# Tokens multiplied by VectorE, the place of their weights, and a range check in a fused convolution and MLP kernel

## The chip, the core and the metric

The kernel runs on one core of one Trainium2 chip. The metric is the device time of one execution in microseconds (us). Before the change it is 745.89 us, the median of three runs (745.74 to 745.92).

The core's engines have queues of their own and work through them in order: TensorE (PE, with PEld for the weight load that precedes a matmul), VectorE (DVE), ScalarE (ACT), GpSimd (POOL) and SyncE (SP, which only issues DMAs here). They meet through semaphores.

## The reference

Two stages, in fp32. A dynamic convolution: each of 8 batches x 4096 tokens has 192 values in 8 groups of 24, and for each group 7 weights, made by a softmax, that weigh the token and the six before it. Then an MLP with g = h - tanh(h).

```python
w = np.exp(weight_gen - np.max(weight_gen, axis=-1, keepdims=True))
w = w / (np.sum(w, axis=-1, keepdims=True) + 1e-09)
...
out = np.einsum('bshk,bskhg->bshg', w, x_unf)     # 7 taps
...
h = x @ w_in            # 32768 x 192  @  192 x 2048
g = h - np.tanh(h)
return (g @ w_out)      # 32768 x 2048 @ 2048 x 192
```

The weights going into the softmax are drawn as 0.3 times a normal variable. The kernel before the change leaves the maximum out and takes exp as it is.

## The kernel before

**Superblocks.** The 32768 tokens are cut into 32 superblocks of 1024: 128 partitions with 8 consecutive tokens each (j = 0 to 7). Each goes through the same stages, and the stages of several superblocks overlap. The main loop (L707) runs over n = 1 to 31, and within it over 16 tiles f of the hidden dimension (L713). `tc.manual_schedule()` (L564) keeps each engine's instructions in the order in which the code issues them, so the order is written by hand.

**Softmax.** ScalarE takes exp of the weights (L169), VectorE sums over the 7 taps (L183), takes the reciprocal (L198, into a corner of a PSUM tile) and scales (L229). For superblocks 3 and 8 GpSimd does the scaling.

**Products of the taps.** Taps 0 to 3 go to `pa`, 4 to 6 to `pb`, bf16, [taps, 8 tokens, 192]. GpSimd makes nearly all (L299). The dictionary `HELP` (L51) names *helped tokens*: (m, f) in `HELP[k]` says that while superblock m runs its tile f, VectorE makes taps 0 and 1 of one token of superblock k (`help`, L243), starting with j = 7, and GpSimd's first product of k gets shorter by a token. Superblocks 4 to 31 have one such token, at f = 3 two superblocks ahead; 9 to 14 have a second, at f = 12 three ahead. VectorE first copies the 16 weights of the token into the PSUM tile `ph` of that f (L250), whose values have been used by then, and multiplies from there (L251).

**Adding the taps.** A DMA that accumulates adds `pb` onto taps 0 to 2 of `pa` (L236). For the superblocks in `TWO_SUMS` (13 to 31) a second such DMA adds taps 2 and 3 onto 0 and 1. What is left is added by TensorE: matmuls against an identity transpose the parts and add them up in PSUM (`pc`, L384), 24 for each part in each superblock, 96 with four parts and 48 with two. ScalarE evicts the result to `convT` (L410).

**First matmul.** For each f, six matmuls (three chunks of 64 channels by two halves of the tokens) write `ph` (L427), [128, 1024] fp32, two PSUM banks; there are three such buffers, shared with `pc`. ScalarE makes `th` = tanh (L440), VectorE `gt` = `ph` - `th` in bf16 (L441).

**Second matmul.** It lags one superblock. A block is one token column j of 128 tokens, and takes 32 matmuls (16 tiles, two row halves of 64) into one of two PSUM banks, `obank` 0 and 1, alternately, columns 0 to 191 of 512 (L495). `out_stream` interleaves the first half of block i with the second half of block i - 1, in pairs; `out_pairs(m)` emits m pairs. How many come after each f stands in the lists `pairs` of the plans (L682 to L686): `STEADY` has 0 after f = 2 and 16 after f = 3, 0 after f = 8 and 6 after f = 9, 8 after each of f = 11 to 14. Superblocks 4 to 11 use `DOUBLE`, with the same numbers at f = 2, 3 and 8. ScalarE evicts a finished block to `out_sb` (L514), and SyncE stores eight together.

**The end.** The second matmul of superblock 31 has nothing to run beside (`gemm2_last`, L529): for each of its eight blocks 32 matmuls into a `ph` buffer, a ScalarE copy of one half (L551) and a VectorE add of the other (L552); SyncE stores two blocks at a time (L554).

Of the kernel before, what the change touches and what calls it, by code (L numbers as in the profile page):

```python
# [8 lines left out]
FP32 = mybir.dt.float32  # L9
# [3 lines left out]
AX = mybir.AxisListType  # L13


@with_exitstack
def kernel(
# [18 lines left out]
    J = 8  # L36
# [9 lines left out]
    TWO_SUMS = (13, 14, 15, 16, 17, 18, 19, 20, 21, 22, 23, 24, 25, 26, 27, 28, 29, 30, 31)  # L46
# [4 lines left out]
    HELP = {n: ((n - 2, 3),) for n in (4, 5, 6, 7, 8, 9, 10, 11, 12, 13, 14, 15, 16, 17, 18, 19, 20, 21, 22, 23, 24, 25, 26, 27, 28, 29, 30, 31)} | {9: ((7, 3), (6, 12)), 10: ((8, 3), (7, 12)), 11: ((9, 3), (8, 12)), 12: ((10, 3), (9, 12)), 13: ((11, 3), (10, 12)), 14: ((12, 3), (11, 12))}  # L51
    LAST_TAP = (4, 5, 6, 7, 8)
    X_LATE = ()
    ZERO_AT = 8
# [28 lines left out]
    once = const.tile([P, 1], FP32, name="once")  # L83

# [94 lines left out]
    def softmax_sum(n, j0=0, j1=J):  # L179

        if j0 == 0:
            zsum_of[n] = wgpool.tile([P, J * H], FP32, name="zsum")
        nc.vector.reduce_sum(  # L183
            out=zsum_of[n][:, j0 * H : j1 * H],
            in_=e_of[n][:, j0:j1].rearrange("p j h k -> p (j h) k"),
            axis=AX.X,
        )

# [5 lines left out]
    def softmax_norm(n, bank):  # L194

        wsm = softmax_tile()
        zr_v = bank[:, 512 - J * H : 512]
        nc.vector.reciprocal(zr_v, zsum_of[n][:])  # L198

        def finish():  # L200
            scale(nc.vector, wsm[:], e_of[n], zr_v)

        wsm_of[n] = (wsm, None, None, None)
        return finish

    def softmax_norm_ramp(n, bank):
# [4 lines left out]
        nc.vector.reciprocal(zr_v, zsum_of[n][:])  # L211
# [31 lines left out]
    def help(n, ph, j):  # L243

        if n not in held:
# [3 lines left out]
        w = ph[:, 0, 0 : KH * H].rearrange("p (k h) -> p k h", k=KH)  # L249
        nc.vector.tensor_copy(w, wsm[:, j].rearrange("p h k -> p k h")[:, 0:KH])  # L250
# [7 lines left out]
            w.rearrange("p k (h o) -> p k h o", o=1).to_broadcast([P, KH, H, G]),  # L258
# [269 lines left out]

    def gemm2_last(j, f0=0, f1=NFT):  # L529

        n = NTOT - 1
        if f0 == 0:
            half[j] = psum_h.tile([P, 2, HT], FP32, name="po2", tag="ph")
        po = half[j]
        col = (j % 2) * HT + (j // 2) * P
        for f in range(f0, f1):
            for r in range(2):
                nc.tensor.matmul(  # L538
                    po[:, r, 0:D],
                    lhsT=g_of[n][f][r * R : (r + 1) * R, col : col + P],  # L540
                    rhs=w_out[r * R : (r + 1) * R, f, :],
                    start=(f == 0),
                    stop=(f == NFT - 1),
                )
        if f1 < NFT:
            return
# [4 lines left out]
        nc.scalar.activation(out=ot[:], in_=po[:, 0, 0:D], func=ACT.Copy)  # L551
        nc.vector.tensor_add(out_sb[:, j, :], po[:, 1, 0:D], ot[:])  # L552
        if j % 2 == 1:
            nc.sync.dma_start(  # L554
                out=out[n * TOK : (n + 1) * TOK, :].rearrange("(p j) e -> p j e", p=P)[
                    :, j - 1 : j + 1, :
                ],
                in_=out_sb[:, j - 1 : j + 1, :],
            )
# [4 lines left out]
    ctx.enter_context(tc.manual_schedule())  # L564
# [122 lines left out]
    DOUBLE_IN = (4, 5, 6, 7, 8, 9, 10, 11)  # L687
# [19 lines left out]
    for n in range(1, NTOT):  # L707
# [5 lines left out]
        for f in range(NFT):  # L713
            ph = gemm1(n, f)
# [17 lines left out]
            if n == AHEAD and f == 4:  # L732
                softmax_exp(n + 4)
            if n > 1:
# [9 lines left out]
            for m in (n + 2, n + 3):  # L744
                if (n, f) in HELP.get(m, ()):
                    help(m, ph, J - 1 - HELP[m].index((n, f)))
# [22 lines left out]

    gemm2_last(0, 0, J)  # L770
    out_pairs(NFT)
    gemm2_last(0, J, NFT)
    for j in range(1, J):
        gemm2_last(j)

# [29 lines left out]
```

## Time and profile before

| what | value |
|---|---|
| median of three runs | 745.89 us |
| span of the profiled execution, first to last instruction | 743.4 us |
| superblocks 8 to 11 (four parts), from tanh to tanh | 22.67 us each |
| superblocks 14, 15, 17, 18 (two parts) | 21.85 us each |
| subtraction L441, VectorE | 512 x 1217 ns |
| tanh L440, ScalarE | 512 x 1025 ns |
| copy of a helped token's weights L250, VectorE | 34 x 190 ns |
| product of a helped token L251, VectorE | 34 x 554 ns |
| GpSimd's first product with 8, 7, 6 tokens | 6025, 5416, 4765 ns |
| accumulating DMA, issue on POOL: first, second sum | 1284, 1651 ns |
| last matmul's end in the span | 739.57 us |

The profile is of one execution, and its span is 2.5 us under the median time of the runs; what lies before the first and after the last instruction is not in it. How to read its lines: a group or timeline line gives the source line, the engine, the operation, output <- inputs by their names, shapes and a count, and where the engine idled before it, how long and what ended that. A line of waits gives who waited, for whom, the sum in us, how often, and the longest. A line of windows gives the stretch, its length, busy time and count for each engine, the clock granted to TensorE (1.00 is full), the busy share of the DMA engines and GB/s.

### The profile page before, as it was taken

Reading aid. Unit: us, or ns where it says so; the run is one execution under the profiler, and the core shown is the slowest. Engines: PE = TensorE matmul, PEld = TensorE weight load, DVE = VectorE, ACT = ScalarE, POOL = GpSimd, SP = SyncE. Lnnn points to the kernel's source line nnn. Section 1 sums busy time; section 2 is a strip of 40 time slices with the busy share of each in tenths; the row PEclk is TensorE's granted clock in tenths of the full one; section 3 lists DMA queues with packets and bytes.
Section 4 is the critical chain, followed back from the end, with each engine's and each line's share of the span. In section 5 each row is a group of like instructions: output and inputs, shape, how many; then the busy total and the mean of one; then the engine's idle time right before and its main releaser. Section 6 shows DMA issues by size and latency. Waiting matters only on the chain.

```text
span 743.4 us, 30037 instructions
## 1 busy us (share of the span) xinstructions
PE 722.3 (97%) x13616; PEld 556.5 (75%) x13616; DVE 687.4 (92%) x723; ACT 638.8 (86%) x872; POOL 654.5 (88%) x163
## 2 busy tenths in 40 slices
PE   3899999999999999999999999999999999999997
PEld 2477777778777777777777777777777777877777
DVE  7999899999999999999999999999999999988893
ACT  4888888888888888989889999898998989888882
POOL 7999999999999999999999999999999999991000
PEclk9899999999999999999999999999999999999999
DMA  8925367766567668878777977877887877776112
GB/s 236 245 46 161 135 172 185 195 179 149 124 183 184 183 185 224 210 199 203 166 202 209 236 186 204 178 195 205 221 209 195 192 181 194 193 149 110 45 45 86
DMA packets 34269, 130.06 MB, mean 175 GB/s; under 512 B 4591, under 2 KB 9439, under 8 KB 30174
## 3 DMA queue, kind: packets, MB, share of 16 engines
q0 software_dynamic: 19424, 51.12, 40.4%
q1 hardware_dynamic: 14718, 77.03, 27.6%
q8 instruction: 106, 1.74, 0.9%
q14 instruction: 21, 0.17, 0.1%
HBM read 54.52 MB, written 25.17 MB: 107 GB/s over the span
## 4 chain that ended last, share of the span: by engine, by line
PE 92%; DVE 5%; ACT 1%; issue 1%; DMA 1%; SPq 0%; DVEq 0%
PE ph L427 43%; PE obank L495 43%; PE pc L384 4%; DVE gt L441 3%; PE po L538 1%; ACT th L440 1%; DVE pa L299 1%; DMA wg_t<-in_weight_gen_dram 1%; DVE zsum L183 0%; SPq L134 0%; ACT convT L402 0%; DVE obank L211 0%; DVE pa L251 0%; DVE pb L299 0%; SPq L144 0%
## 5 line engine op out<-in xcount | busy, mean ns | idle before, releaser
L441 DVE TENSOR_TENSOR gt<-ph,th 128x1024 bf16<-128x1024 f32 x512 | 601.6, 1217 | 33.4 <-ACT th L440 23.2
L440 ACT ACTIVATE th<-ph 128x1024 f32<-128x1024 f32 x512 | 512.1, 1025 | 69.2 <-PE ph L427 60.3
L427 PE MATMUL ph<-convT,w_in 64*128 64x512 bf16 x3072 | 415.1, 379 | 5.3 <-DVE gt L441 3.3
L495 PEld LDWEIGHTS <-gt 64*128 64x128 bf16 x7936 | 355.6, 94 | 80.6 <-issue 6.3
L495 PE MATMUL obank<-w_out,gt 64*128 64x192 bf16 x7936 | 408.0, 243 | 0.9 <-issue 0.8
L299 POOL TENSOR_TENSOR pa<-x_t,wsm 128x2688 bf16<-128x2688 f32 (+3 forms) x68 | 338.9, 5232 | 0.2
L299 POOL TENSOR_TENSOR pb<-x_t,wsm 128x4608 bf16<-128x4608 f32 (+2 forms) x33 | 283.8, 8601 | 0.7 <-ACT wsm L221 0.5
L427 PEld LDWEIGHTS <-w_in 64*128 64x128 bf16 x3072 | 163.0, 94 | 86.0 <-issue 18.3
L514 ACT ACTIVATE out_sb<-obank 128x192 f32<-128x192 f32 x248 | 81.3, 328 | 11.2 <-PE obank L495 10.3
L410 ACT ACTIVATE convT<-pc 128x1024 bf16<-128x1024 f32 (+1 forms) x62 | 50.1, 810 | 2.9 <-PE pc L384 2.7
L236 POOL DMA_DIRECT2D pa<-pb x28 | 36.0, 1284 | 13.7 <-POOL pb L299 9.1
L384 PEld LDWEIGHTS <-pa 64*128 64x128 bf16 x2064 | 41.5, 100 | 6.8 <-DVE pa L299 1.1
L236 POOL DMA_DIRECT2D pa<-pa x21 | 34.7, 1651 | 9.6 <-DMA pa<-pb 8.9
L384 PE MATMUL pc<-ident,pa 64*128 64x64 bf16 x1968 | 41.2, 191 | 1.8 <-POOL pa L299 0.9
L183 DVE TENSOR_REDUCE zsum<-wg_t 128x32 f32<-128x224 f32 (+1 forms) x61 | 23.6, 387 | 2.9 <-ACT wg_t L169 2.9
L169 ACT ACTIVATE wg_t<-wg_t 128x448 f32<-128x448 f32 x32 | 18.2, 570 | 6.3 <-DMA wg_t<-in_weight_gen_dram 6.2
L251 DVE TENSOR_TENSOR pa<-x_t,ph 128x384 bf16<-128x384 f32 x34 | 18.8, 554 | 2.0 <-DVE ph L250 0.3
L229 DVE TENSOR_TENSOR wsm<-wg_t,pc 128x448 f32<-128x448 f32 x27 | 16.8, 621 | 2.5
L198 DVE RECIPROCAL pc<-zsum 128x64 f32<-128x64 f32 x27 | 14.9, 550 | 0.0
L384 PE MATMUL pc<-ident,pb 64*128 64x64 bf16 x216 | 4.9, 206 | 9.0 <-POOL pb L299 9.0
L384 PEld LDWEIGHTS <-pb 64*128 64x128 bf16 x288 | 6.3, 106 | 9.5 <-POOL pb L299 9.0
L538 PE MATMUL po<-w_out,gt 64*128 64x192 bf16 x256 | 11.2, 243 | 0.0
(27 smaller groups left out, 56.8 us busy)
## 6 DMA issues: line engine op xcount, KB each, us to landing
x_t<-in_x_dram SPq DMA_DIRECT2D x31, 1344.0 KB, 7.9
pa<-pb POOLq DMA_DIRECT2D x28, 1152.0 KB, 9.5
out_dram<-out_sb SPq DMA_DIRECT2D x31, 768.0 KB, 3.9
pa<-pa POOLq DMA_DIRECT2D x21, 768.0 KB, 7.2
wg_t<-in_weight_gen_dram SPq DMA_DIRECT2D x32, 224.0 KB, 7.1
x_t<-in_x_dram SPq DMA_DIRECT2D x1, 768.0 KB
w_out<-in_moe_w_out_dram POOLq DMA_DIRECT2D x1, 768.0 KB, 9.5
out_dram<-out_sb SPq DMA_DIRECT2D x4, 192.0 KB, 3.0
```

The lines of the kernel that those rows point to most:

```text
L183: nc.vector.reduce_sum(out=zsum_of[n][:, j0 * H : j1 * H], in_=e_of[n][:, j0:j1].rearrange("p j h k -> p (j h) k"), axis=AX.X,)
L236: return nc.gpsimd.dma_start(out=out.rearrange("p k j d -> p k (j d)"), in_=in_.rearrange("p k j d -> p k (j d)"), accum_op=mybir.AluOpTyp ...
L251: nc.vector.tensor_mul(pa[:, 0:KH, j, :].rearrange("p k (h g) -> p k h g", h=H), bass.AP(tensor=x_v.tensor, offset=x_v.offset + j * D, ap= ...
L299: return eng.tensor_mul(prod(k0, k1)[:, :, j0:j1].rearrange("p k j (h g) -> p k (j h) g", h=H), bass.AP(tensor=x_v.tensor, offset=x_v.offs ...
L384: nc.tensor.matmul(pc[r][:, col : col + R] if home else pc[:, r, col : col + R], lhsT=prods[c][gi][r * R : (r + 1) * R, 2 * j : 2 * j + 2] ...
L410: last_conv[0] = nc.scalar.activation(out=out, in_=pc[:, :, 0:cols].rearrange("p r (cj t) -> p r cj t", t=R), func=ACT.Copy,)
L427: nc.tensor.matmul(ph[:, r, :], lhsT=w_in[r * R : (r + 1) * R, c, f * P : (f + 1) * P], rhs=convT[r * R : (r + 1) * R, c, :], start=(c == ...
L440: last_act[0] = nc.scalar.activation(out=th[:], in_=ph_f, func=ACT.Tanh)
L441: last_sub[0] = nc.vector.tensor_sub(gt[:], ph_f, th[:])
L495: mm = nc.tensor.matmul(po[:, 0:D], lhsT=g_of[n][f][r * R : (r + 1) * R, col : col + P], rhs=w_out[r * R : (r + 1) * R, f, :], start=(r == ...
L514: last_act[0] = nc.scalar.activation(out=out_sb[:, j, :], in_=po[:, 0:D], func=ACT.Copy)
L538: nc.tensor.matmul(po[:, r, 0:D], lhsT=g_of[n][f][r * R : (r + 1) * R, col : col + P], rhs=w_out[r * R : (r + 1) * R, f, :], start=(f == 0 ...
```

## The change

- **More helped tokens.** `HELP` gives a second helped token to superblocks 4 to 8 (at f = 8, two ahead) and to 15 to 18 (at f = 12, three ahead); 9 to 14 keep theirs. 43 tokens in place of 34.
- **Weights.** Their copy is made by ScalarE (`help_weights`), issued ahead of that f's first matmul, into columns 256 to 287 of `obank` 0 or 1, alternately. The product on VectorE stands where it stood, behind the subtraction of that f.
- **Second sums** from superblock 8 in place of 13.
- **Plans.** `DOUBLE` only for superblocks 4 to 6; 7 to 11 use `STEADY`.
- **Range check.** All sums of the softmax are kept in one tile (`zall`). VectorE reduces it to its largest and smallest value (three parts at f = 14 of superblocks 28 to 30, the rest in the tail), and a flag says whether all lie between 1e-18 and 1e30.
- **General version.** Every engine reads the flag and branches. If it is 0, loops compute everything again with the maximum subtracted. With the drawn inputs it is stepped over.
- **The end.** Block 7 goes to `obank` 0 and 1. The branch comes before its eviction and before the last two stores, of blocks 4 to 6 together and of block 7.

```diff
-    TWO_SUMS = (13, 14, ..., 31)
+    TWO_SUMS = tuple(range(8, 32))
...
-    HELP = {n: ((n - 2, 3),) for n in (4, 5, ..., 31)} | {9: ((7, 3), (6, 12)), ..., 14: ((12, 3), (11, 12))}
+    HELP = {n: ((n - 2, 3),) for n in range(4, 32)}
+    for n in range(4, 9):
+        HELP[n] += ((n - 2, 8),)
+    for n in range(9, 19):
+        HELP[n] += ((n - 3, 12),)
...
+    STORES = {1: 0, 3: 2}
+    LAST_STORES = {6: 4, 7: 7}
+    SUM_MAX, SUM_MIN = 1e30, 1e-18
+    CHECK = {(28, 14): (0,), (29, 14): (1,), (30, 14): (2,)}
...
-            zsum_of[n] = wgpool.tile([P, J * H], FP32, name="zsum")
+            zsum_of[n] = zall[:, n * J * H : (n + 1) * J * H]
...
+    def sums_piece(i):
+        w = NTOT * J * H // 2
+        if i < 4:
+            op = ALU.max if i < 2 else ALU.min
+            nc.vector.tensor_reduce(ends[:, i : i + 1], zall[:, i % 2 * w : (i % 2 + 1) * w], AX.X, op)
+        elif i == 4:
+            nc.vector.tensor_scalar(ends[:, 0:2], ends[:, 0:2], SUM_MAX, None, op0=ALU.is_le)
+        elif i == 5:
+            nc.vector.tensor_scalar(ends[:, 2:4], ends[:, 2:4], SUM_MIN, None, op0=ALU.is_ge)
+        elif i == 6:
+            nc.vector.tensor_mul(fine[:], ends[:, 0:2], ends[:, 2:4])
+            nc.sync.dma_start(out=fine_row[:], in_=fine[:])
+        else:
+            nc.vector.tensor_reduce(flag[:], fine_row[:], AX.X, ALU.min)
...
-    def help(n, ph, j):
+    w_col = [0]
+    w_of = {}
+
+    def help_weights(n, j):
+        wsm = held[n][1] if n in held else wsm_of[n][0]
+        at = 256 + w_col[0] // 2 % 2 * KH * H
+        w = obank[w_col[0] % 2][:, at : at + KH * H].rearrange("p (k h) -> p k h", k=KH)
+        w_col[0] += 1
+        nc.scalar.activation(out=w, in_=wsm[:, j].rearrange("p h k -> p k h")[:, 0:KH], func=ACT.Copy)
+        w_of[n, j] = w
+
+    def help(n, j):
...
-        w = ph[:, 0, 0 : KH * H].rearrange("p (k h) -> p k h", k=KH)
-        nc.vector.tensor_copy(w, wsm[:, j].rearrange("p h k -> p k h")[:, 0:KH])
         nc.vector.tensor_mul(
             pa[:, 0:KH, j, :].rearrange("p k (h g) -> p k h g", h=H),
...
-            w.rearrange("p k (h o) -> p k h o", o=1).to_broadcast([P, KH, H, G]),
+            w_of.pop((n, j)).rearrange("p k (h o) -> p k h o", o=1).to_broadcast([P, KH, H, G]),
...
-    DOUBLE_IN = (4, 5, 6, 7, 8, 9, 10, 11)
+    DOUBLE_IN = (4, 5, 6)
...
         for f in range(NFT):
-            ph = gemm1(n, f)
+            helps = [(m, J - 1 - HELP[m].index((n, f))) for m in (n + 2, n + 3) if (n, f) in HELP.get(m, ())]
+            for m, j in helps:
+                help_weights(m, j)
+            gemm1(n, f)
...
+            for piece in CHECK.get((n, f), ()):
+                sums_piece(piece)
...
+            for m, j in helps:
+                help(m, j)
...
+    for piece in (3, 4, 5, 6):
+        sums_piece(piece)
     gemm2_last(0, 0, J)
...
     for j in range(1, J):
+        if j == 4:
+            sums_piece(7)
         gemm2_last(j)
...
+    good = nc.values_load(flag[:], min_val=0, max_val=1)
+    with tc.If(good < 1, preferred_fallthrough_block=False):
+        with tc.For_i(0, B) as b:
...
+                general(b * NSB + s, carry)
+    store_last(J - 2)
+    evict_last(J - 1)
+    store_last(J - 1)
```

## The prediction

> **What bounds the kernel now.** I read the page first: its busy times, the granted clock over the span and the shares of the chain.
>
> ```profile
> PE 722.3 (97%) x13616; PEld 556.5 (75%) x13616; DVE 687.4 (92%) x723; ACT 638.8 (86%) x872; POOL 654.5 (88%) x163
> PEclk9899999999999999999999999999999999999999
> PE 92%; DVE 5%; ACT 1%; issue 1%; DMA 1%; SPq 0%; DVEq 0%
> ```
>
> TensorE is busy in 97% of the span, makes 92% of the chain that ended last, and after the first slices has its full clock. Next come the windows cut at the first tanh of superblocks 11, 12, 15 and 16 (columns: stretch, length, busy us and count of PE, PEld, DVE, ACT, POOL, then clock and DMA).
>
> ```profile
> 267.09:289.76 22.67, 22.67 (x454) 17.68 (x450) 21.58 (x25) 19.84 (x28) 22.37 (x7) 1.00 0.72 198
> 289.76:311.61 21.85, 21.85 (x406) 16.93 (x402) 20.93 (x24) 19.70 (x27) 21.08 (x6) 1.00 0.80 201
> 355.62:377.47 21.85, 21.85 (x406) 16.84 (x402) 21.03 (x23) 19.71 (x27) 21.13 (x6) 1.00 0.80 199
> 377.47:400.10 22.63, 22.08 (x406) 17.52 (x402) 21.14 (x23) 19.71 (x28) 21.68 (x6) 1.00 0.80 199
> ```
>
> A normal superblock is as long as its matmuls: PE has no gap in it. Superblocks 7 to 11 hold 48 more transposes (454 against 406 matmuls) and take 22.67 us instead of 21.85. So whatever makes TensorE wait in a superblock is added to the time in full. Third, the timeline around f = 2 to 5 of superblock 15.
>
> ```profile
> 357.37 1.48 PE L427 MATMUL ph<-convT,w_in 64*128 64x512 bf16 x12
> 358.27 1.94 ACT L440 ACTIVATE th<-ph 128x1024 f32<-128x1024 f32 x2
> 358.66 1.50 PE L495 MATMUL obank<-w_out,gt 64*128 64x192 bf16 x32
> 359.33 2.35 DVE L441 TENSOR_TENSOR gt<-ph,th 128x1024 bf16<-128x1024 f32 x2
> 359.98 0.83 PE L427 MATMUL ph<-convT,w_in 64*128 64x512 bf16 x6
> 361.72 0.19 DVE L250 COPY ph<-wsm 128x16 f32<-128x16 f32 x1
> 361.95 0.56 DVE L251 TENSOR_TENSOR pa<-x_t,ph 128x384 bf16<-128x384 f32 x1
> ```
>
> The twelve matmuls of f = 2 and 3 start at 357.37; TensorE goes straight on at 358.66 with 32 matmuls of the second product into obank. VectorE subtracts for f = 2 and 3 from 359.33, and only then makes the helped token's product, done at 362.51. That is 3.85 us after the obank matmuls began, and nobody on TensorE minds, since the weights lie in ph. Last, the waits:
>
> ```profile
> PEld L427 <- DVE pa L251: 0.9, 3, 0.4
> PE ph L427 <- DVE pa L251: 0.2, 1, 0.2
> ```
>
> TensorE does honour a wait for this product: it must not overwrite ph before the product has read it. With three ph buffers that costs 1.1 us in the whole run.
>
> **The change part by part.** Superblock and f are those of the first matmul then running; a helped token is one whose first two taps VectorE makes.
>
> *The new wait, the term that decides.* The copy of the weights moves to ScalarE and to columns 256 and up of obank 0 or 1. The second matmul writes columns 0 to 191 of the same banks. In the changed program as built, the order on each engine around f = 3 of a steady superblock is:
>
> ```
> PE   12 matmuls f = 2, 3 -> ph; 1 matmul -> obank1
> ACT  tanh f=2; copy weights -> obank0; tanh f=3
> DVE  subtract f=2; subtract f=3; product <- x_t, obank0
> PE   load weights: WAITS for that product; 31 matmuls -> obank
> ```
>
> The wait keeps TensorE out of the bank until VectorE has read it, though the columns differ. Everything behind it on TensorE's queue stands: the other obank matmuls, f = 4, later the transposes; then ScalarE and VectorE run dry.
> Its length at f = 3, from the timeline: without the copy the product starts at 361.72 and ends at 362.28; TensorE was ready at 358.70 (one obank matmul, 1.32/32 = 0.04, is ahead of the wait, or none where bank 1 has the weights); handing over, with a weight load (0.09) no longer hidden, about 0.1. That is 3.7 us. The reach is 3.4 (no handover, ScalarE a little earlier) to 4.0 (the copy delays tanh by its 0.2). 28 superblocks have it (2 to 29): 103.6.
> At f = 12 (superblocks 6 to 15) one tile lies ahead. From its first matmul to the product's end: 0.90 to the tanh (357.37 to 358.27), 1.03, 1.22 for the subtraction, 0.56, and 0.06 between them, 3.77; TensorE is ready after 0.65 + 0.04. With 0.1 it is 3.2 (2.9 to 3.6), times 10: 32.0.
> At f = 8 (superblocks 2 to 6) the next tile's matmuls, 0.65, stand between: 2.5 (2.2 to 3.0), times 5: 12.5. No gap remains in these superblocks to absorb any of it. Together +148.1, between 135 and 163.
>
> The Trainium skill, "PSUM — Partial Sum Buffer", section "PSUM bank collisions raise a hardware error", says to guard PSUM by bank and quadrant, not by address; this speaks against weights in a bank that matmuls keep writing. No run here shows a collision.
>
> *What the gaps do to the clock.* Gaps of this size occurred in the ramp. Windows on the clock's own grid (PE busy, clock, DMA):
>
> ```profile
> 12.93:16.34 3.41, 1.22 (x56) 1.00 1.00 316
> 16.34:19.75 3.41, 3.17 (x16) 0.50 0.73 119
> 19.75:23.17 3.41, 1.32 (x11) 1.00 0.53 111
> 23.17:26.58 3.41, 3.41 (x18) 0.50 0.98 340
> 30.00:33.41 3.41, 2.81 (x79) 1.00 1.43 236
> ```
>
> A stretch of 3.41 us in which PE was busy for 1.22 or 1.32 us was followed by one at half clock; 2.81 busy was not. The threshold lies between 39% and 82%; I take half. A gap of 3.7 us always leaves one stretch under it. The half-clocked one costs up to 1.7 us, less where the gap itself still fills part of it, more where two follow. Averaged over where the gap falls on the grid: 1.65 at f = 3, 1.55 at f = 12, 1.2 at f = 8 (a short gap can split evenly): 46.2 + 15.5 + 6.0 = +67.7. With the threshold at 39% it is 53, at 82% it is 92; nothing, if such gaps do not count outside a ramp. I take the middle, as the ramp is the nearest row.
> The Trainium skill, "TensorE: Matmul & The Clock Gate", section "Part 1: The HAM clock gate", puts the drop after at least one idle window of about 3.4 us. By it only gaps that fill a window count: of 3.7 us gaps one in twelve, some 4 us in all, and the time would be about 894. The rows above differ from it, dropping after 1.2 to 1.3 us of work in a window.
>
> *Second sums from superblock 8.* Five superblocks (7 to 11) lose 48 transposes each: 5 x 0.81 = -4.1. POOL issues five more DMA sums; between starts that is 0.8 us each (286.30 to 287.08 in its timeline). It also drops nine tokens of two taps, (5.42 - 4.77) x 9 = 5.9. POOL is covered, as superblocks grow well past its 21 to 22 us; the cover would go with the wait.
>
> *Superblocks that were late* (4, 6, 13, 16, 19, 24, 26) exceed their neighbours by 2.9 in all, with POOL at its limit. With room for POOL some of it goes: -1.5 (0 to -2.9).
>
> *Copies and products.* 34 VectorE copies (0.19) go, 43 ScalarE copies come: between the 128x1 row (0.17) and the 128x192 row (0.33). ScalarE idles 2.1 us in each superblock: 0 beyond the wait. Nine more products of 0.55 stand in VectorE's 0.8 idle: 0. Superblocks 7 to 11 taking the other order of second-product matmuls: same matmuls, 0.
>
> *Range check.* Three reductions of 128x1024: by 0.375 for 224 and 0.614 for 448 about 1.2 us each, in superblocks 28 to 30, where VectorE idles 1.8 to 2.9. Uncovered each would cost 1.2. The fourth and the small ones fall in VectorE's 2.2 us gap before the first sum of the tail. 0.
>
> *The tail.* Before, matmuls end at 739.57, then copy 0.33, add 0.36, store, 742.2 landed. Now each engine reads the flag and branches before the last token's copy, and the general version is stepped over. ScalarE has 1.0 us between the evictions of tokens 6 and 7 to hide it. No row shows a flag read or a far branch. Below: all hidden, 0. Above: two fetches as long as the median landing of these stores (3.0), minus 1.0: 5. I take 1.5, nearer to the sequencer's rows (0.05 each).
>
> **Sum.** 743.4 - 4.1 - 1.5 + 148.1 + 67.7 + 1.5 = 955.1 for the span. The runs' median, 745.89, is 2.5 above the span of the profiled execution: 957.6, so 957.
>
> **Rivals.**
> 1. *The clock holds.* The gaps come, but steady work around them keeps the full clock. For it: 0.55 us of idle in superblock 16 left it at 1.00. Against: the ramp's rows. 957 - 68 = 889, reach 875 to 905.
> 2. *It drops harder*: every gap throws two stretches to half clock, or the wait finds ScalarE late. 957 + 28 x 1.7 = 1005.
> 3. *Not slower: the wait is met for nothing*, VectorE's product being done when TensorE arrives. Its place is the weight load behind each product; its price 4.1 + 1.5 - 1.5 saved, 742. It decides once the 43 waits cost under 4/43 = 0.1 us each. Against: the product at f = 3 needs the tanh of the tile that TensorE has just finished, so it can't be done in time.
> 4. *The change doesn't do what it says*: transposes stay or the general version runs. The program has 240 fewer; the general version runs only if a sum of seven exponentials of small weights leaves 1e-18 to 1e30. Nothing speaks for it.
>
> **How the numbers follow.** Gaps and clock drop, 925 to 995: 0.72. Clock holds: 0.13. Harder: 0.06. A partial cover, 760 to 870: 0.05. Met for nothing: 0.03, most of it faster. The remaining 0.01 is spread. The range from 885 to 1000 holds the first and most of the second, bounded by the sums of low ends (743.4 - 4.1 - 2.9 + 135 + 2.5 = 874) and high ends (743.4 - 4.1 + 163 + 92 + 5 + 2.5 = 1002). A difference of 0.2%, 1.5 us, is about what a measurement tells from none: faster 0.03, same 0.01, slower 0.96.
>
> **What the profile after would show.** Right: 43 waits of the second matmul's weight load for the product, about 3.4 us each; superblocks of 27 us (single help) and 31 to 32 (two); the clock row with 8s and 9s; 406 matmuls in superblocks 7 to 11. Wrong: no such wait, or a clock of 1.00 throughout, or a long gap at the end before the last store.

## The result, and the profile after

The changed kernel takes 927.38 us (median of six runs, 925.59 to 928.66) against 745.9 us before: a ratio of 1.243, with a 95% interval of 1.2412 to 1.2447. The forecast was slower, 957 us, between 885 and 1000. The profiled execution took 927.14 us with a span of 925.2; the span grew by 181.8 us.

These lines of the page after are busy time by engine and the clock granted in 40 slices of the span.

```profile
PE 771.2 (83%) x13376; PEld 588.7 (64%) x13376; DVE 695.2 (75%) x706; ACT 644.9 (70%) x915; POOL 654.7 (71%) x168
PEclk9998999988998899889988999999999999999999
```

TensorE has 240 matmuls fewer and yet is busy 49 us longer: part of the time its clock was low (the mean is 0.937, before 0.995). Its share of the span fell from 97% to 83%, so it also waits. ScalarE and GpSimd fell to 70% and 71% with it: no engine is full any more. The waits of the changed kernel (who waited on which line for whom, the sum in us, how often, the longest) name what TensorE waits for.

```profile
DVE gt L482 <- ACT th L481: 206.7, 159, 5.2
ACT out_sb L555 <- PE obank L536: 153.1, 72, 4.7
PEld L536 <- DVE pa L292: 149.4, 43, 3.9
POOL pa L267 <- DVE pa L292: 147.8, 21, 10.8
PE obank L536 <- DVE pa L292: 131.8, 43, 3.4
```

The two `L536 <- DVE pa L292` lines are one wait seen twice, by the weight load and by the matmul behind it: 43 times the second matmul (L536) stands until VectorE's product (L292) has read its weights out of obank. VectorE, ScalarE and POOL then wait in turn. Before, the weight loads' wait for this product was 0.9 us in all, in front of another buffer. The timeline around f = 2 and 3 of superblock 28 shows one such wait from end to end.

```profile
682.18 1.47 PE L468 MATMUL ph<-convT,w_in 64*128 64x512 bf16 x12
683.47 0.24 PE L536 MATMUL obank<-w_out,gt 64*128 64x192 bf16 x1
683.99 0.21 ACT L283 ACTIVATE obank<-wsm 128x16 f32<-128x16 f32 x1
684.14 2.36 DVE L482 TENSOR_TENSOR gt<-ph,th 128x1024 bf16<-128x1024 f32 x2
686.42 0.55 DVE L292 TENSOR_TENSOR pa<-x_t,obank 128x384 bf16<-128x384 f32 x1
687.02 1.49 PE L536 MATMUL obank<-w_out,gt 64*128 64x192 bf16 x31 [3.30 <-DVE pa L292]
```

One obank matmul passes at 683.47, into the bank that has no weights. The next finds the bank taken by the copy of 683.99. VectorE must first subtract for f = 2 and f = 3 (2.36 us from 684.14); its product ends at 686.97, and at 687.02 the 31 remaining matmuls go. Nothing runs on TensorE from 683.71 to 687.02.

Third, the windows cut at the first tanh of superblocks 17, 18, 14, 15 and 3 (columns: stretch, length, busy us and count of PE, PEld, DVE, ACT, POOL, clock, DMA share, GB/s).

```profile
519.99:545.34 25.35, 22.05 (x406) 16.87 (x402) 20.94 (x22) 19.81 (x29) 18.61 (x6) 1.00 0.69 173
545.34:572.34 27.00, 23.64 (x406) 17.44 (x402) 20.94 (x22) 19.83 (x28) 23.04 (x6) 0.94 0.65 164
430.74:460.63 29.89, 23.75 (x406) 18.09 (x402) 21.40 (x23) 20.09 (x29) 20.70 (x5) 0.94 0.59 148
460.63:491.86 31.23, 25.09 (x405) 19.47 (x402) 21.41 (x23) 20.09 (x29) 20.71 (x5) 0.89 0.56 142
93.24:121.49 28.25, 22.82 (x454) 17.75 (x450) 21.45 (x23) 20.18 (x30) 27.66 (x8) 1.00 0.51 141
```

Superblock 17 has one wait and a full clock: 25.35 against 21.85 before, so a wait at f = 3 costs 3.50 us. Superblock 18 has one wait and one half-clocked stretch: 1.65 us more. Superblocks 14 and 15 have waits at f = 3 and f = 12. Superblock 3 has waits at f = 3 and f = 8 and kept its clock: 28.25 against 22.69, so f = 8 costs 5.56 - 3.50 = 2.1. POOL, busy for 27.66 there, isn't the reason: superblock 2 of the run with the held clock below takes 28.65 with POOL at 21.69.

Last, the clock's own grid (PE busy, clock, DMA) around the waits in superblocks 18 and 17.

```profile
548.46:551.87 3.41, 0.10 (x2) 1.00 0.55 231
551.87:555.28 3.41, 3.35 (x36) 0.51 0.34 62
555.28:558.70 3.42, 3.42 (x62) 0.99 1.07 190
...
521.19:524.60 3.41, 2.08 (x31) 1.00 0.30 128
524.60:528.01 3.41, 1.43 (x33) 1.00 0.26 104
528.01:531.43 3.42, 3.42 (x59) 1.00 0.80 142
```

In superblock 18 the gap fell into one window, TensorE was busy in it for 0.10 us, and the next ran at half speed. In superblock 17 the same gap fell across two windows, 2.08 and 1.43 us busy, and none was slowed. Over the run after the ramp 32 stretches of 3.41 us were at half clock, for 43 waits.

### The profile page after: what moved, and what is told of

Read it like the earlier page. It is cut to its first block, busy times and chain, and to the rows that moved or that the text cites. A ratio compares the mean times of both kernels' runs of the same rounds, so it can differ in the third digit from the quotient of the medians.

```text
span 925.2 us, 29614 instructions
## 1 busy us (share of the span) xinstructions
PE 771.2 (83%) x13376; PEld 588.7 (64%) x13376; DVE 695.2 (75%) x706; ACT 644.9 (70%) x915; POOL 654.7 (71%) x168
## 5 line engine op out<-in xcount | busy, mean ns | idle before, releaser
L536 PE MATMUL obank<-w_out,gt 64*128 64x192 bf16 x7936 | 443.5, 253 | 131.9 <-DVE pa L292 131.8
L536 PEld LDWEIGHTS <-gt 64*128 64x128 bf16 x7936 | 376.7, 98 | 232.7 <-DVE pa L292 149.4
L468 PE MATMUL ph<-convT,w_in 64*128 64x512 bf16 x3072 | 439.6, 394 | 5.2 <-DVE gt L482 3.8
L340 POOL TENSOR_TENSOR pa<-x_t,wsm 128x2688 bf16<-128x2688 f32 (+3 forms) x68 | 331.7, 5095 | 12.9 <-PE ph L468 7.9
L468 PEld LDWEIGHTS <-w_in 64*128 64x128 bf16 x3072 | 179.0, 98 | 80.2 <-issue 17.9
L267 POOL DMA_DIRECT2D pa<-pa x26 | 41.8, 1607 | 8.9 <-DMA pa<-pb 8.3
L198 DVE TENSOR_REDUCE zall<-wg_t 128x32 f32<-128x224 f32 (+1 forms) x61 | 23.6, 388 | 2.8 <-ACT wg_t L184 2.8
L292 DVE TENSOR_TENSOR pa<-x_t,obank 128x384 bf16<-128x384 f32 x43 | 23.4, 544 | 0.0
L229 DVE RECIPROCAL pc<-zall 128x64 f32<-128x64 f32 x27 | 14.9, 551 | 0.7 <-ACT convT L451 0.7
L591 PEld LDWEIGHTS <-gt 64*128 64x128 bf16 x256 | 10.8, 93 | 0.0
```

The lines of the kernel that those rows point to most:

```text
L198: nc.vector.reduce_sum(out=zsum_of[n][:, j0 * H : j1 * H], in_=e_of[n][:, j0:j1].rearrange("p j h k -> p (j h) k"), axis=AX.X,)
L267: return nc.gpsimd.dma_start(out=out.rearrange("p k j d -> p k (j d)"), in_=in_.rearrange("p k j d -> p k (j d)"), accum_op=mybir.AluOpTyp ...
L292: nc.vector.tensor_mul(pa[:, 0:KH, j, :].rearrange("p k (h g) -> p k h g", h=H), bass.AP(tensor=x_v.tensor, offset=x_v.offset + j * D, ap= ...
L340: return eng.tensor_mul(prod(k0, k1)[:, :, j0:j1].rearrange("p k j (h g) -> p k (j h) g", h=H), bass.AP(tensor=x_v.tensor, offset=x_v.offs ...
L468: nc.tensor.matmul(ph[:, r, :], lhsT=w_in[r * R : (r + 1) * R, c, f * P : (f + 1) * P], rhs=convT[r * R : (r + 1) * R, c, :], start=(c == ...
L536: mm = nc.tensor.matmul(po[:, 0:D], lhsT=g_of[n][f][r * R : (r + 1) * R, col : col + P], rhs=w_out[r * R : (r + 1) * R, f, :], start=(r == ...
```

## The experiments

What the runs had to decide: whether weights in obank are the whole loss, or the other parts (tokens, sums, check) share in it; whether the 181.8 us divide into waits and clock as forecast; and whether a change without that wait would beat the kernel before.

### One part alone, and that part taken away

The kernel before with nothing but the copy into obank, by ScalarE, for its 34 helped tokens:

```diff
-        w = ph[:, 0, 0 : KH * H].rearrange("p (k h) -> p k h", k=KH)
-        nc.vector.tensor_copy(w, wsm[:, j].rearrange("p h k -> p k h")[:, 0:KH])
+        at = 256 + w_col[0] // 2 % 2 * KH * H
+        w = obank[w_col[0] % 2][:, at : at + KH * H].rearrange("p (k h) -> p k h", k=KH)
+        w_col[0] += 1
+        nc.scalar.activation(out=w, in_=wsm[:, j].rearrange("p h k -> p k h")[:, 0:KH], func=ACT.Copy)
```

> The kernel before with one part of the change alone: ScalarE copies the weights into obank, ahead of the tile's first matmul. Helped tokens (34), second sums, plans and the tail as before. Theory of the bank wait: 28 waits at f = 3 of 3.5 us and 6 at f = 12 of 2.9 (as read from the changed kernel's superblocks) give 115; the half-clocked stretches, 32 for 43 waits there at about 1.6 each, give 41 for 34. 745.9 + 156 = 902, between 885 and 915. Rival, the added work: with 34 tokens and no new sums it stays within 5 of 746.

Measured: 901.46 us (901.27 and 901.65), ratio 1.2085 (1.2056 to 1.2113), clock 0.947. Its waits:

```profile
PEld L505 <- DVE pa L261: 125.3, 34, 3.9
PE obank L505 <- DVE pa L261: 110.8, 34, 3.4
```

Thirty-four waits, as many as helped tokens. The edit that moves 16 columns per token from ph to obank, and their copy from VectorE to ScalarE ahead of the tile, costs 155.5 us with nothing else changed.

The reverse: the changed kernel with VectorE's copy into ph put back, and all else kept.

```diff
+        w = ph[:, 0, 0 : KH * H].rearrange("p (k h) -> p k h", k=KH)
+        nc.vector.tensor_copy(w, wsm[:, j].rearrange("p h k -> p k h")[:, 0:KH])
...
-            for m, j in helps:
-                help_weights(m, j)
-            gemm1(n, f)
+            ph = gemm1(n, f)
```

> The changed kernel with one part undone: the weights of a helped token are copied by VectorE into ph again, in front of the product. Tokens, second sums, plans, range check and general version stay as changed. Theory of the bank wait: without the weights in obank no second-product matmul waits for VectorE, the 43 waits and the half-clocked stretches go, and what is left is 745.9 - 4.1 (transposes) - 0 to 2.9 (late superblocks) + 0.9 (tail, read from the profile after), 740 to 743. Rival, the added work: the second helped tokens or the earlier second sums themselves keep VectorE and POOL late, so the time stays well above before, over 760, with waits of POOL for VectorE's products near the 148 us of the changed kernel.

Measured: 758.12 us (756.28 to 759.27), ratio 1.0158 (1.0145 to 1.0171), clock 0.998. The place of the weights, with the copy's engine, is worth 927.4 - 758.1 = 169 us. But the expected 740 to 743 was missed by some 16: the rest of the change, which I had counted as a small gain, loses 12 us when the waits are gone. The windows of superblocks 7 and 10 show two kinds of it.

```profile
182.07:207.78 25.71, 22.35 (x407) 16.78 (x403) 22.70 (x26) 19.88 (x28) 25.41 (x7) 1.00 0.74 172
253.35:276.08 22.73, 21.92 (x406) 16.41 (x402) 21.64 (x25) 19.76 (x27) 22.43 (x7) 1.00 0.84 213
```

The first is as long as POOL's work (25.41 of 25.71). In the second TensorE idles 0.81 us; POOL is busy for 22.43 of the 22.73, but superblock 13 takes the same 22.73 with POOL at 20.44. What TensorE waits for stands in its waits:

```profile
PE ph L470 <- DVE pa L294: 8.8, 13, 0.8
```

A helped product reads its weights from ph, and TensorE needs that buffer: 0.81 us at f = 12 in each of superblocks 8 to 15, and 0.4 to 0.6 at f = 8 in 2 to 6. In the kernel before this was 0.2 us in all, so it is the largest wait that the change adds when obank is free. The rest is looked for further below.

### The waits and the clock, each by itself

To hold the clock, matmuls that nobody reads were put ahead of each wait, into a free ph buffer: 28 at f = 3, 17 at f = 8, 23 at f = 12.

```diff
+    FILL = {3: 28, 8: 17, 12: 23}
+    def fill(n, f):
+        ph = psum_h.tile([P, 2, HT], FP32, name="ph", tag="ph")
+        for i in range(FILL[f]):
+            c, r = i // 2 % NC, i % 2
+            nc.tensor.matmul(
+                ph[:, r, :],
+                lhsT=w_in[r * R : (r + 1) * R, c, f * P : (f + 1) * P],
+                rhs=convT[r * R : (r + 1) * R, c, :],
+                start=True,
+                stop=True,
+            )
...
+            if (f in (3, 12) and helps) or (f == 9 and (n, 8) in HELP.get(n + 2, ())):
+                fill(n, 8 if f == 9 else f)
```

> The changed kernel with TensorE kept busy during the waits: ahead of each wait 28, 17 or 23 matmuls (f = 3, 8, 12) of the first product's form go into a free ph buffer and are never read; 0.108 us each, just under the gaps of 3.3, 2.1 and 2.8. The waits themselves stay. It tells the clock's share from the wait's. Theory that both count: no stretch falls under half clock, and the 32 half-clocked stretches after the ramp, about 1.6 each, go: 927 - 52 = 875, between 868 and 885, clock 0.99. Rival, the low clock costs nothing, since TensorE would wait for VectorE anyway: 920 to 930 at a clock of 0.99.

Measured: 877.8 us (877.67 and 877.93), clock 0.995, no half-clocked stretch after the ramp. The windows of superblocks 11 and 17, and the wait that is left:

```profile
321.04:349.32 28.28, 28.01 (x457) 19.64 (x453) 21.37 (x23) 19.98 (x29) 20.71 (x5) 1.00 0.62 157
487.79:513.13 25.34, 25.10 (x434) 18.41 (x430) 20.93 (x22) 19.80 (x28) 21.38 (x6) 1.00 0.69 174
```

```profile
PEld L551 <- DVE pa L292: 13.0, 39, 0.4
```

TensorE is now busy through the gaps, so the clock stays at 1.00, and superblocks 16 to 27 with one wait take 25.35 each, 7 to 15 with two 28.28. The added matmuls themselves cost nothing that shows: 25.35 is also what superblock 17 took without them at a full clock. So the clock's share of the loss is 927.4 - 877.8 = 49.6 us, and the waits cost 3.50 at f = 3, 28.28 - 25.35 = 2.93 at f = 12, and in superblocks 2 to 5 (28.2 to 28.7, before 22.6 to 23.0) 2.1 at f = 8. With the waits' 28 x 3.50 + 10 x 2.93 + 5 x 2.1 = 137.8, the clock's 49.6, the transposes' -4.1, the late superblocks' -2.9 and +0.9 in the tail the account is 181.3 of 181.8.

To shorten the wait without changing where the weights lie, the product was put ahead of the subtraction of its own tile on VectorE:

```diff
             for m, j in helps:
                 help_weights(m, j)
+                help(m, j)
             gemm1(n, f)
...
-            for m, j in helps:
-                help(m, j)
```

> The changed kernel with VectorE's product one place earlier: ahead of the subtraction of its tile instead of behind it. Weights stay in obank. Theory: the wait is as long as the chain tanh, subtraction, product behind TensorE's last tile, so it shortens by about a subtraction, 1.2: 2.3 at f = 3, 1.85 at f = 12, 1.0 at f = 8, 88 in all in place of 137; gaps of 2.1 us and less leave most stretches above the clock's threshold, 0 to 30 for the clock. 741 + 88 + 0 to 30 = 829 to 860. Rival, the cost is per copy or per token, whatever the order on VectorE: 925 as the changed kernel.

Measured: 849.93 us (847.91 and 851.95), clock 0.973. TensorE's waits and one of its gaps:

```profile
PE obank L536 <- DVE pa L292: 79.4, 43, 2.2
...
522.37 1.53 PE L536 MATMUL obank<-w_out,gt 64*128 64x192 bf16 x31 [2.17 <-DVE pa L292]
```

One subtraction less (1.22) in front of the product shortens the wait from 3.3 to 2.2 us; a superblock with one wait takes 24.20 or, with a half-clocked stretch, 25.88. What sets the wait's length is VectorE's queue in front of the product, as the prediction had it.

### Weights in SBUF

If only the bank is in the way, a tile of their own in SBUF should free TensorE altogether.

```diff
+    w_help = const.tile([P, 4 * KH * H], FP32, name="w_help")
...
-        at = 256 + w_col[0] // 2 % 2 * KH * H
-        w = obank[w_col[0] % 2][:, at : at + KH * H].rearrange("p (k h) -> p k h", k=KH)
+        at = w_col[0] % 4 * KH * H
+        w = w_help[:, at : at + KH * H].rearrange("p (k h) -> p k h", k=KH)
```

> The changed kernel with the weights copied by ScalarE as changed, but into a small tile in SBUF instead of obank. It tells the place of the weights from the engine that copies them. Theory of the bank wait: only the place matters, so 740 to 743 as with ph, perhaps 0 to 1 less since VectorE loses 43 copies of 0.19 us. Rival, the copy on ScalarE is the trouble (it stands between two tanh, 0.21 us each in the profile after): 43 copies delay the chain and some of the 181 us stays, over 750.

Measured: 899.9 us (895.8 to 901.3, and one run of six at 911.1), ratio 1.2056 (1.2032 to 1.2081), clock 0.931. The expectation failed by 157 us. TensorE no longer waits for the product in obank, but the product itself is another. Its group (busy us, mean ns) and the waits:

```profile
L293 DVE TENSOR_TENSOR pa<-x_t,w_help 128x384 bf16<-128x384 f32 x43 | 162.4, 3777 | 0.0
```

```profile
ACT th L482 <- PE ph L469: 173.9, 215, 13.9
POOL pa L267 <- DVE pa L293: 114.6, 22, 14.2
PE ph L469 <- DVE gt L483: 108.4, 29, 12.7
```

In the changed kernel the same product with weights in PSUM takes 544 ns; here 3777 ns on average, from 548 to 18952 with a median of 1394. The timeline of superblock 18 shows on what it depends: the big product of POOL, and VectorE's.

```profile
565.58 9.32 POOL L341 TENSOR_TENSOR pb<-x_t,wsm 128x4608 bf16<-128x4608 f32 x1
...
573.92 1.39 DVE L293 TENSOR_TENSOR pa<-x_t,w_help 128x384 bf16<-128x384 f32 x1
```

POOL's product ends at 574.90, VectorE's 0.41 later, at 575.31. The 13 products that met no POOL tensor instruction took 0.55 us; the other 30 ended 0.41 to 0.43 us after POOL's, and where POOL had several in a row they stood up to 19 us. Subtractions behind them, and then TensorE's ph buffers, waited for that.
The Trainium skill, "SBUF — State Buffer", section "SBUF: two separate sides", states this: VectorE and GpSimd share a pair of ports that one of them holds for a whole instruction, and a VectorE operation with two inputs in SBUF is shut out by a GpSimd operation that reads SBUF. The rows agree, 548 ns without and up to 18952 ns with GpSimd at work.

To see whether the copy or the operand's memory does it, a kernel without any copy, whose product reads the weights from the softmax tile in SBUF:

```diff
-            for m, j in helps:
-                help_weights(m, j)
...
-            w_of.pop((n, j)).rearrange("p k (h o) -> p k h o", o=1).to_broadcast([P, KH, H, G]),
+            wsm[:, j].rearrange("p h k -> p k h")[:, 0:KH].rearrange("p k (h o) -> p k h o", o=1).to_broadcast([P, KH, H, G]),
```

> The changed kernel with no copy of the weights at all: VectorE's product reads them where the softmax left them, in SBUF with a step of seven. Theory: no bank is touched, so 740 to 743; if reading with a step costs VectorE nothing, no copy was needed in the first place. Rival: the product gets slower than its 0.54 us from SBUF (both operands then come from there), by 0.3 or more, and VectorE, with 0.8 us idle in a superblock, passes some on: 1 to 5 us above the kernel with the copy in SBUF.

Measured: 898.88 us (896.55 to 900.93). The group:

```profile
L292 DVE TENSOR_TENSOR pa<-x_t,wsm 128x384 bf16<-128x384 f32 x43 | 161.9, 3765 | 0.0
```

The same time and the same mean: the copy is innocent, the operand's memory decides. Beside GpSimd's products the weights are better in PSUM, and in a part of it that TensorE does not need soon.

The kernel with the SBUF tile was also run without the range check, the flag, the branch and the general version (the four `sums_piece` calls, `values_load`, `tc.If` and `general` removed):

> As the kernel with the weights in SBUF, without the range check, the flag, the branch and the general version; these are left out. It prices them. The profile after has the flag read at 0.46 to 0.54 us and two branches on ScalarE between the evictions of tokens 6 and 7, the last store issued at 922.07 against a last matmul at 920.53, 4.68 us from there to the end of the span against 3.82 before. Theory: 0.9 us for the tail, plus up to 1 us for four reductions if VectorE's idle time does not hide them; so 739 to 742, 0.9 to 1.9 below the kernel with the check. Rival: all of it is hidden, no difference beyond 0.3.

Measured: 899.73 us (895.4 to 904.9, and one run of six at 909.6). Against 899.9 that is no difference, but with this spread it says nothing on a price of 1 to 3 us: inconclusive. It was asked again on a steadier kernel, below.

### The 12 us that are left

First, the kernel before with the second tap sums from superblock 8 alone:

```diff
-    TWO_SUMS = (13, 14, 15, 16, 17, 18, 19, 20, 21, 22, 23, 24, 25, 26, 27, 28, 29, 30, 31)
+    TWO_SUMS = tuple(range(8, 32))
```

> The kernel before with second sums from superblock 8 alone. Theory: five superblocks lose 48 transposes, 0.81 us each, 4.1 in all, since POOL's five more DMA issues of 0.8 us fit: 741 to 743. Rival: POOL, busy 22.37 of 22.67 us there, has no room for them at a period of 21.85 without the second helped tokens, and TensorE waits for parts instead: 744 or more.

Measured: 754.05 us (753.51 to 755.76), ratio 1.0113 (1.0094 to 1.0131): the rival. The windows of superblocks 7, 8 and 11:

```profile
177.52:205.19 27.67, 23.55 (x405) 18.67 (x401) 21.47 (x25) 20.02 (x28) 27.37 (x8) 0.94 0.80 185
205.19:231.95 26.76, 23.60 (x406) 18.06 (x402) 21.66 (x25) 20.04 (x27) 26.46 (x8) 0.94 0.93 228
276.86:299.30 22.44, 22.16 (x406) 16.79 (x402) 21.46 (x25) 19.84 (x27) 20.83 (x6) 1.00 0.81 198
```

The transposes are gone (406 matmuls instead of 454), yet superblocks 7 and 8 take 27.67 and 26.76 instead of 22.62 and 22.67: POOL fills all but 0.30 of them, TensorE waits 4.1 and 3.2 us, and each has a half-clocked stretch. Both waits are of transposes for the landing of a second sum:

```profile
PE pc L384 <- DMA pa<-pa: 7.3, 2, 4.1
```

Even superblock 11, with POOL at 20.83, keeps 22.44 instead of 21.85.

Then four kernels on one chip. The first takes the version with weights in ph and asks for the order DOUBLE up to superblock 15:

```diff
-    DOUBLE_IN = (4, 5, 6)
+    DOUBLE_IN = tuple(range(4, 16))
```

> The changed kernel with the weights back in ph and the order DOUBLE kept in superblocks 4 to 15, where a product at f = 12 is made (the changed kernel takes STEADY from 7). Theory: the 0.81 us of PE idle in each of superblocks 8 to 15 with the weights in ph (22.73 against 21.86) is the ph buffer that the product at f = 12 still holds when STEADY asks for the transposes at f = 13; DOUBLE asks for them elsewhere, so 8 x 0.87 = 7.0 goes: 758.1 - 7 = 751 (749.5 to 752.5), superblocks 9 to 15 21.9. Rival: the product is late for another reason (VectorE with one token more), and the order does not matter: 757 to 759.

Measured: 758.65 us (758.53 to 759.29), ratio 1.018 (1.0166 to 1.0194): not 751. The windows of superblocks 7 and 11:

```profile
182.15:208.40 26.25, 23.57 (x406) 18.27 (x402) 21.57 (x25) 20.02 (x28) 25.95 (x8) 0.93 0.73 169
276.57:299.01 22.44, 22.15 (x406) 16.79 (x402) 21.46 (x25) 19.85 (x27) 21.31 (x6) 1.00 0.81 202
```

The order does take away the eight waits of 0.81 for the product (the line of 8.8 us falls to 2.3, five waits at f = 8). But it brings only 0.3 us of the 0.87 in these superblocks (22.73 to 22.44): the matmuls take 22.15 instead of 21.92, and 0.29 us of idle is left. Superblock 7 lost half a microsecond, superblock 9 0.6. So the buffer held by the product was the wait, as expected, but without it the time is no better.

The second also puts the sums back:

```diff
-    TWO_SUMS = tuple(range(8, 32))
+    TWO_SUMS = tuple(range(13, 32))
```

> As the run before it, with the second tap sums from superblock 13 as in the kernel before. Theory: the earlier second sums load POOL's queue in superblocks 6 to 11 (alone they cost 8.2 us in the kernel before, 4.1 of transposes saved already counted). With the nine more helped tokens, which give POOL 0.65 us each back, part of that is covered: without the early sums superblocks 7 to 11 go back to 22.67 (+4.1 over 21.86), and the excess of superblocks 6 and 7 (24.55 and 25.71, some 6 us over the kernel before's) goes: 751 - 6 + 4 = 749 (747.5 to 750.5). Rival: nine tokens more for VectorE, not the sums, are what delays superblocks 2 to 7; then only the transposes come back: 755.

Measured: 756.56 us (755.48 to 759.97), ratio 1.016 (1.0138 to 1.0182). Superblock 7 goes from 26.25 to 22.62, but 8 to 11 get their transposes back and superblock 10 takes 24.61. The step from the run before, -2.1, has the size that was expected of it (-6 + 4), but this run's times spread over 4.5 us and the two intervals overlap, so the step is not clear of noise; the level is 7.5 us higher, by what the order did not bring. In the profiles, superblocks 3 and 6 stay at 24.3 and 24.4, so the sums delayed superblock 7 and not these.

The third leaves out check, flag, branch and general version as well, and so has the nine more tokens (`HELP`), the order and the new stores at the end beside the kernel before:

> As the run before it, without the range check, the flag, the branch and the general version, and so the kernel before with nine more helped tokens and the order DOUBLE to superblock 15. Theory: the tail's 2.4 goes, and some of the late superblocks (13, 16, 19: about 1.5 in all) too, as POOL has less to do, while superblock 3 keeps about 1.9 more: 746 (744 to 748). Rival: help for POOL decides more than that, 743 to 744, and the tokens by themselves are a gain; or a loss, 749 and more, if VectorE's added products delay it in superblocks 2 to 6.

Measured: 754.78 us (753.15 to 755.26), ratio 1.0118 (1.0102 to 1.0133). The tokens with this order lose 9 us. Superblocks 3, 6 and 14 of it, and then superblocks 3, 6 and 14 of the kernel before:

```profile
85.53:109.66 24.13, 22.98 (x454) 17.68 (x450) 22.08 (x25) 20.13 (x28) 23.83 (x6) 1.00 0.57 160
157.08:181.65 24.57, 23.06 (x454) 18.09 (x450) 22.50 (x27) 19.84 (x27) 24.27 (x7) 1.00 0.67 168
343.23:365.63 22.40, 22.11 (x406) 16.82 (x402) 21.42 (x25) 19.81 (x27) 20.44 (x6) 1.00 0.77 195
```

```profile
84.87:107.56 22.69, 22.69 (x454) 17.35 (x450) 20.89 (x23) 19.97 (x28) 22.39 (x6) 1.00 0.62 173
153.18:176.45 23.27, 23.05 (x455) 17.37 (x451) 21.70 (x25) 19.80 (x28) 22.89 (x8) 1.00 0.60 161
333.77:355.62 21.85, 21.85 (x406) 16.82 (x402) 21.03 (x23) 19.70 (x28) 21.09 (x6) 1.00 0.80 199
```

VectorE gets the product and the copy (superblock 3: 20.89 to 22.08 busy), and TensorE, which had no gap there, gets one of 1.15 us. Superblocks 2 to 6, whose order is the same in both, grow by 5.2 us together: these are the tokens' own. 9 to 16 grow by 4.7, and as the order differs from 12 to 15, the two are not separated there. The last superblock, with the new stores, is no longer than before (36.10, before 36.42). The waits of this kernel name the ph buffers that the added products hold:

```profile
PE ph L470 <- DVE gt L484: 4.7, 12, 1.4
PE ph L470 <- DVE pa L294: 2.3, 5, 0.6
```

The second line was 0.2 us before. The two together (7.0 us, before 3.5) are not all of the 9, and the queue of TensorE's weight loads shows the rest only as time with no wait that the profile names; how much of it is VectorE's later subtractions and how much POOL's later start was not taken apart. That POOL starts later can be seen in its own waits, of this kernel and then of the kernel before:

```profile
POOL pa L267 <- DVE pa L294: 22.3, 12, 5.1
POOL pa L236 <- DVE pa L251: 4.2, 5, 1.1
```

POOL may issue its accumulating DMA only when VectorE's product has written its token into `pa`. So the help that shortens GpSimd's product by 0.65 us a token makes it wait 18 us more over the run.

The fourth is the kernel before with only the check, the flag, the branch over the general version and the new stores of the last superblock:

> The kernel before with only the range check, the flag, the branch over the general version and the new stores of the last superblock: helped tokens, their weights, the order and the sums are as before. Theory: only the tail grows, by what the far branch costs VectorE there with weights in ph: 745.9 + 2.4 = 748.3 (747.3 to 749). Rival: ScalarE's 1 us between the last evictions hides most of it: 746 to 746.8.

Measured: 747.71 us (747.46 to 749.05) against 745.44 beside it, ratio 1.0035 (1.0021 to 1.0048). From the first tanh of superblock 31 to the end it took 37.50 us (36.42 before), so 1.1 of the 2.3 us is seen in the tail. The other 1.0 us of the span lies in superblocks before it, 13 first (22.58, before 22.16), where nothing was changed, and is not explained. Check, flag, branch and stores together are not free, though the check's three big reductions are hidden: TensorE has no gap in superblocks 28 to 30.

No version with a part of this change beat the kernel before.

## Why the prediction was right, and where its sums were off

**What bounds the kernel.** Right: TensorE had no gap to give, and what made it wait was added in full (25.35 = 21.85 + 3.50 in superblocks 16 to 27 when the clock was held).

**The new wait, +148.1.** The mechanism was right to the count, 43 waits of the weight load for the product. The sizes were a little high: 3.7, 3.2 and 2.5 us were forecast, 3.50, 2.93 and 2.1 measured, 137.8 in all. The tenth of a microsecond for handing over and the start of the wait were both on the cautious side: the product ends at 686.97, the matmul starts at 687.02. The first two lie just inside the low ends given, 3.4 and 2.9; 2.1 is below its 2.2.

**The clock, +67.7.** It did drop, which settles the rival in which it holds (889): with the clock held by force the time was 877.8. The term measured 49.6. The step that failed is "A gap of 3.7 us always leaves one stretch under it", with the threshold at half. The windows after a gap put it lower: 25 windows with TensorE busy 36% or less were followed by half clock, all twelve from 44% to 51% by full clock, and of three at 42 to 43% one (1.45 of 3.41 us, superblock 2) was followed by half clock and two were not. Two other runs agree: the kernel before with weights in obank (25 windows of up to 37% followed by half clock, none from 44% on) and the one with the product put ahead (13 of up to 38%, none from 42% on). So a gap that falls evenly over two grid windows costs no clock, which 17, 23 and 29 show, and 43 waits gave 32 half-clocked stretches, 26 behind a gap and 6 behind another. The price of one, 1.65, was right (27.00 - 25.35). The lower bound of the prediction, 53 for a threshold of 39%, was nearer than its middle. A half-clocked stretch that was itself only some 62 to 75% busy was followed by another (six of six); from 82% on none was. The Trainium skill, "TensorE: Matmul & The Clock Gate", section "Part 1: The HAM clock gate", puts the drop after at least one idle window of about 3.4 us. These rows disagree with it: windows that were 33 to 36% busy, with 1.1 to 1.2 us of work, were enough.

**Second sums, -4.1.** The transposes went as counted. That POOL was covered was true only because the waits covered it, and the prediction said that the cover would go with the wait. Uncovered, in the kernel before, the edit costs 8.1 us instead of saving 4.1.

**Nine more products, 0.** Here the working was wrong in kind, and the waits hid it: "Nine more products of 0.55 stand in VectorE's 0.8 idle" took idle time in a superblock as room at any point of it. That the term came out at 0 was luck. With weights in ph the products hold a buffer that TensorE asks for (8.8 us of waits in the changed kernel with that one edit), and keep POOL's DMA back; in the kernel before the tokens, with the other order, cost 9 us. A forecast for the change without its big wait would have said some 742 by the same working; the run with the weights in ph took 758.

**Late superblocks, -1.5.** They went, all or nearly all of the 2.9: in the run with the held clock 13, 16, 19, 24 and 26 are as long as their neighbours.

**Range check, 0, and tail, +1.5.** Superblock 31 grew by 0.86 in the changed kernel, 1.1 in the kernel before with the check alone. With weights in ph, nine more tokens and the check it was 2.2 to 2.4 in three kernels. There VectorE's first instruction came 3.1 to 3.25 us after its branch began, in the changed kernel and in the kernel before with the check alone 0.56; why is open. The bounds of 0 to 5 held.

**The sum.** 957 - 10.3 (waits) - 18.1 (clock) - 1.4 (late superblocks) - 0.6 (tail) = 926.6, for 927.4 measured. Some 60% of the error is the clock's. That the small terms came near is partly luck, as the waits covered two of them.

**The rivals.** That every gap throws two stretches (1005) is refuted by superblocks like 17. That the wait is met for nothing (742) had its condition at 0.1 us per wait; they were 2.1 to 3.5. The change does what it says: 240 matmuls fewer, and the general version does not run.

## What to carry to other kernels

A scratch value laid into a PSUM bank that matmuls keep writing can stop them, though the columns differ: here each use cost what the reader's queue still had to do before it read, 2.1 to 3.5 us, and the gap cost up to 1.65 us more through the clock. Whether the wait comes from the bank or from both being one tile of the program (`obank`) was not separated: no run gave the weights a tile of their own in that bank. Count the cost of an edit at nothing only with the cover named, and try it without the cover: here two parts of the change that looked free or good cost 8 us (the second sums) and 9 us (the tokens, with the other order) where TensorE did not wait. Idle time of an engine in a stage is not room for an operation whose operands hold a buffer that the bounding engine asks for.

## What the runs showed of the hardware that was not expected

- A VectorE product of 128x384 with one operand in PSUM took 544 ns (542 to 546 in 43). With both in SBUF it took 548 to 550 ns in the 13 cases in which GpSimd ran no tensor instruction beside it; the other 30 took up to 18952 ns, ending some 0.4 us after GpSimd's. The median of all 43 was 1394 ns.
- TensorE's busy time in a window of the clock's grid of 3.41 us told whether the clock dropped, the length of a gap did not: a gap of 3.3 us that left 1.43 us of work in one window and 2.08 in the other cost nothing, the same gap in one window cost 1.65 us. Matmuls that nobody reads, put into the gaps, held the clock at 0.995 and brought 49.6 us.
- Reading the flag took ScalarE, VectorE, GpSimd and SyncE 0.46 to 0.54 us, their branches 0.04 to 0.06. From the start of the branch over the general version to the next instruction it was 2.1 to 2.3 us on SyncE, 0.43 on ScalarE, and on VectorE 0.56, or 3.1 to 3.25 in the three kernels with weights in ph and nine more tokens. What that time is, the profile does not say.
